# Causal masks carried by the shift and decay matmuls, the early expert table made in PSUM, and a new order of the attention steps

## Chip, cores and metric

One core of a Trainium2 chip runs the whole program. The metric is the device time of one execution in microseconds, lower is better. The kernel before takes 850.12 us (median of 3 runs, 849.7 to 854.04).

## What is computed

Eight batches of eight heads, 576 positions, head size 64, all in float32, then a mixture of eight experts over the 4,608 tokens, each token going to one expert:

```python
scores = scale * np.matmul(q, k.transpose(0, 1, 3, 2))
cum = np.cumsum(log_f, axis=-1)
decay = cum[:, :, :, None] - cum[:, :, None, :]
causal = np.triu(np.ones((S, S), dtype=bool), k=1)
scores = np.where(causal, -1000000000.0, scores + decay)
scores = scores - np.max(scores, axis=-1, keepdims=True)
attn = np.exp(scores)
attn = attn / (np.sum(attn, axis=-1, keepdims=True) + 1e-09)
return np.matmul(attn, v).astype(np.float32)
...
e_idx = np.argmax(logits, axis=1)
for e in range(E):
    h = np.maximum(x[mask] @ w1[e], 0.0)
    out[mask] = gate_w[mask, None] * (h @ w2[e])
```

## The kernel before

**Attention (class `Attn`)** goes by pairs of heads, 32 pairs, four to a batch. The two heads of a pair stand on partitions 0 to 63 and 64 to 127, so each operand of the scores has 64 rows per head and the matmuls of the two heads are issued in turn. Numbers that need more than one 16-bit or reduced-precision term are split into a high and a low part: `split_hi` (line 397, ACT) and `split_lo` (line 403, POOL) of q and k, `half` (line 651, ACT) and `rest` (line 663, DVE or POOL) of the exponentials.

For a pair, `max_mm` (lines 532 to 552) computes scores with the queries on the partitions, in five blocks of 128 queries laid out in four groups, and `max_red` takes the maximum of each row on DVE (lines 561 to 566). Each group has three kinds of matmuls into one PSUM tile: masks first (line 540: a constant 0/1 matrix `id2` times a table `after` with -1e30 above the diagonal), then the decay (line 546: ones `Cq` times `Sk`, whose rows hold -8 times the cumulated logs in three bfloat16 parts), then q times k (line 551). The maxima are transposed on TensorE (line 572), negated and split on DVE (lines 578, 579), and sent by DMA into rows of `Sq` (`shift_out`, line 586). `scores` (lines 590 to 623) has the keys on the partitions, again masks (line 606, `id2` and `later`), then decay and shift in one matmul of `Sk` and `Sq` (line 613), then three products of q and k parts (line 621). A mask group of a block of 128 columns has a 128-column and a 64-column matmul per head. `exp` (lines 630, 636) follows on ACT; `weighted` (lines 689 to 691) multiplies the exponentials with v, 15 times three matmuls per head; `divide` (lines 700 to 705) normalises. `put_cum` (line 412) sends the cumulated logs of a pair into `Sk` by one DMA from SP, `Sk` and `Sq` having three slots in turn. Per batch there are also the scaling of v, the key gates (line 491), the routing (`route`) and the scatter of the tokens into the experts' lists (`scatter`, line 797, an indirect DMA on POOL).

**The order.** Nothing is scheduled by the compiler here: `steps` lists every step with the steps it comes after and with the PSUM and SBUF rings it takes, and `Plan.order` emits, one by one, the ready step with the smallest due time. A step's due time is `PERIOD * b + DUE[kind][stage][q]`, where the stage is batch 0, batch 1, a middle batch or the last one and q the pair within the batch. The engines then run their instructions in that order. The costs given to `add` are not used by the kernel. The tile `pb` is one PSUM bank that the transposes, the key gates and the small matmuls share.

**Setup.** `Moe.__init__` makes the constants of the experts on POOL before `Attn.setup` makes those of attention on DVE, POOL and ACT, computes the cumulated logs (lines 274 to 301) and splits q and k of the first two pairs. `setup2` follows as a step.

**The early table.** After batch 5 (`EB`), `early` (line 1327) counts the tokens of each expert so far (line 996, TensorE), works out on DVE which expert and which rows the first four tiles take (`first_table`, lines 1062 to 1074, with `parts`, `slots` and `table`) and loads two tiles of x. It is one step, after the scatters of batch 5. `other_tables` does the rest during the experts' stage.

**Experts (class `Moe`)**: 14 to 18 tiles of 256 tokens and up to eight of 128, each with two layers as three products of split operands (lines 1211 and 1237), weights loaded and split per expert.

## Time and profile before

| | |
|---|---|
| median of 3 runs | 850.12 us |
| profiled execution | 849.61 us |
| its span, first to last instruction | 847.8 us |
| TensorE busy (mean granted clock 0.983) | 807.1 us, 95% |
| VectorE (DVE) busy | 627.7 us, 74% |
| ScalarE (ACT) busy | 543.2 us, 64% |
| GpSimd (POOL) busy | 378.7 us, 45% |

Times within the profile are microseconds from the first instruction on. A line number is a line of the kernel. Attention fills the first 375 us or so, the experts the rest. In the lists of instructions the columns are start, duration, engine, line, operation, output<-inputs, tile sizes and a count; an arrow in brackets gives the idle time of the engine before the instruction and what ended it. Consecutive instructions of one kind are merged into one line. Matmuls are pipelined, so that a matmul's duration is longer than its distance to the next one.

### The profile page before, as it was taken

The numbers are of one execution on the slowest core, as the hardware profiler recorded it, in microseconds if no ns is written. First come the engines' busy times: TensorE is split into PE (matmuls) and PEld (weight loads), VectorE is DVE, ScalarE is ACT, GpSimd is POOL, SyncE is SP. The second block draws the span as 40 slices with busy tenths as digits, with TensorE's granted clock in tenths as the row PEclk, the third lists the DMA queues.
The fourth block names the chain that finished last, engine by engine and source line by source line (L and its number), as shares of the span: only waits on it lengthen the run. The fifth ranks groups of instructions, "written<-read, shape, count | busy, mean of one in ns | idle before, by whom it ended". The sixth has DMA issues, their size and how long they took to land.

```text
span 847.8 us, 23444 instructions
## 1 busy us (share of the span) xinstructions
PE 807.1 (95%) x9693; PEld 726.9 (86%) x9693; DVE 627.7 (74%) x1170; ACT 543.2 (64%) x688; POOL 378.7 (45%) x370
## 2 busy tenths in 40 slices
PE   3899999999999999699999999999999999999994
PEld 2689898989898988588999999999999999999873
DVE  8679798989898989877777856666655666566484
ACT  4597889898989897474643654444454445444484
POOL 9386889898989897575433111111000110111110
PEclk9699999999999999899999999999999999999997
DMA  5434353535353533171474731101113421116481
GB/s 171 145 104 140 125 182 116 184 116 180 119 182 116 184 115 108 64 244 58 149 249 157 295 121 51 51 27 49 38 51 137 149 67 50 51 44 207 146 299 30
DMA packets 43016, 107.48 MB, mean 127 GB/s; under 512 B 5391, under 2 KB 5583, under 8 KB 42896
## 3 DMA queue, kind: packets, MB, share of 16 engines
q1 hardware_dynamic: 36192, 84.82, 30.1%
q0 software_dynamic: 6704, 21.02, 6.8%
q8 instruction: 80, 1.31, 0.7%
q14 instruction: 40, 0.33, 0.1%
HBM read 143.14 MB, written 21.80 MB: 195 GB/s over the span
## 4 chain that ended last, share of the span: by engine, by line
PE 86%; DVE 7%; POOL 2%; issue 2%; ACT 1%; DMA 0%; DVEq 0%; POOLq 0%; ACTq 0%
PE ph L1211 23%; PE py L1237 23%; PE ps L621 9%; PE pb L491 4%; PE po L689 4%; PE po L691 3%; PE po L690 3%; PE ps L551 3%; PE ps L613 3%; PE ps L546 2%; PE ph L1293 2%; PE ps L606 2%; PE px L1194 2%; PE ps L540 2%; DVE w1l L1157 1%
## 5 line engine op out<-in xcount | busy, mean ns | idle before, releaser
L1242 POOL DMA_INDIRECT out_dram<-y,xg x36 | 48.0, 1334 | 333.7 <-DVE y L1241 304.8
L1211 PE MATMUL ph<-xh,w1h 128*128 128x256 f32 x576 | 163.3, 284 | 0.3 <-DVE hl L1215 0.3
L1211 PE MATMUL ph<-xl,w1h 128*128 128x256 f32 x576 | 163.1, 283 | 0.0
L1211 PE MATMUL ph<-xh,w1l 128*128 128x256 f32 x576 | 162.9, 283 | 0.0
L663 POOL TENSOR_TENSOR Pl<-Pt,Ph 128x1024 f16<-128x1024 f32 (+1 forms) x63 | 142.0, 2260 | 17.9 <-ACT Ph L651 14.4
L1157 DVE TENSOR_TENSOR w1l<-raw,w1h 128x1024 fp32r<-128x1024 f32 x78 | 97.6, 1265 | 61.5 <-ACT w1h L1155 61.5
L1174 ACT CAST w2h<-raw 128x1024 fp32r<-128x1024 f32 x72 | 74.6, 1048 | 95.1 <-issue 55.3
L1155 ACT CAST w1h<-raw 128x1024 fp32r<-128x1024 f32 x80 | 82.5, 1048 | 82.5 <-PE ph L1211 62.5
L1175 DVE TENSOR_TENSOR w2l<-raw,w2h 128x1024 fp32r<-128x1024 f32 x72 | 87.5, 1221 | 58.7 <-ACT w2h L1174 56.9
L1211 PEld LDWEIGHTS ph<-xh,w1h 128*128 128x128 f32 x576 | 110.5, 192 | 1.2 <-DVE hl L1215 0.5
L1237 PE MATMUL py<-w2h,hh 128*128 128x512 f32 x288 | 111.3, 395 | 0.0
L1211 PEld LDWEIGHTS ph<-xl,w1h 128*128 128x128 f32 x576 | 110.5, 192 | 0.7
L1211 PEld LDWEIGHTS ph<-xh,w1l 128*128 128x128 f32 x576 | 110.5, 192 | 0.0
L1237 PE MATMUL py<-w2l,hh 128*128 128x512 f32 x288 | 110.2, 391 | 0.0
L1237 PE MATMUL py<-w2h,hl 128*128 128x512 f32 x288 | 109.9, 391 | 0.0
L621 PE MATMUL ps<-X 64*128 64x288 f32 (+4 forms) x1152 | 109.8, 319 | 0.0
L689 PE MATMUL po<-vh,Ph 128*128 128x73 f16 x930 | 100.3, 199 | 2.1 <-DVE lgh L705 2.1
L403 POOL TENSOR_TENSOR X<-raw,X 128x1152 fp32r<-128x1152 f32 x32 | 84.7, 2649 | 38.5 <-ACT X L397 38.2
L691 PE MATMUL po<-vh,Pl 128*128 128x73 f16 x930 | 99.8, 198 | 1.5 <-DVE Pl L663 1.3
L690 PE MATMUL po<-vl,Ph 128*128 128x72 f16 x930 | 100.1, 196 | 0.0
L689 PEld LDWEIGHTS <-Ph 128*128 128x128 f16 x960 | 93.6, 98 | 5.9 <-issue 2.8
L636 ACT ACTIVATE Pt<-ps,lnp 128x576 f32<-128x576 f32 (+1 forms) x96 | 81.3, 864 | 24.9 <-PE ps L621 24.9
(301 smaller groups left out, 1944.2 us busy)
## 6 DMA issues: line engine op xcount, KB each, us to landing
raw<-in_w_dram SPq DMA_DIRECT2D x84, 1024.0 KB
raw<-in_qk_dram SPq DMA_DIRECT2D x32, 608.0 KB
vT<-in_vt_dram SPq DMA_DIRECT2D x32, 320.0 KB
xg<-xs SPq DMA_DIRECT2D x18, 514.0 KB
vr<-in_v_dram SPq DMA_DIRECT2D x30, 256.0 KB
raw1b<-in_w_dram SPq DMA_DIRECT2D x4, 1024.0 KB
hxg<-xs SPq DMA_DIRECT2D x5, 257.0 KB
vr<-in_v_dram SPq DMA_DIRECT2D x8, 128.0 KB
```

Source lines behind the costliest of these rows:

```text
L403: e.tensor_tensor(self.two(X[:, 1]), self.two(self.get("raw", p)), self.two(f32(X[:, 0])), ALU.subtract)
L621: nc.tensor.matmul(ps[:, h, c0:c0 + w], X[r, x, k], X[r, y, q], start=False, stop=(j == 2), skip_group_check=True)
L636: nc.scalar.activation(self.get("Pt", (p, i))[:, :, o:o + w], ps[:, :, 0:w], AF.Exp, bias=self.lnp, scale=0.125)
L663: e.tensor_tensor(self.Pl_t[p % 2][:, :, c], self.exps(p, i), self.Ph_t[p % 2][:, :, c], ALU.subtract)
L689: nc.tensor.matmul(o, Ph[:, c0:c0 + P], vh[:, c, hh, :], start=(c == 0), stop=False)
L690: nc.tensor.matmul(o[:, 1:73], Ph[:, c0:c0 + P], vl[:, c, hh, :], start=False, stop=False)
L691: nc.tensor.matmul(o, Pl[:, c0:c0 + P], vh[:, c, hh, :], start=False, stop=(c == ic))
L1155: x = nc.scalar.copy(self.w1h[a], self.raw1[i][a])
L1157: y = e.tensor_tensor(self.w1l[a], self.raw1[i][a], f32(self.w1h[a]), ALU.subtract)
L1175: y = nc.vector.tensor_tensor(self.w2l[a], self.raw2[a], f32(self.w2h[a]), ALU.subtract)
L1211: y = nc.tensor.matmul(ph[:, i, :], w[:, k, f0:f0 + P], x[:, k, :], start=(j == 0), stop=(j == len(m) - 1))
L1237: x = nc.tensor.matmul(py, h[:, k, c * P:c * P + P], w[:, k, :], start=(j == 0), stop=(j == len(m) - 1))
```

## The change

The three mask tables and `id2` go. `Sk` gets three versions of its 128 columns, `Cq` three of its 128 and `Sq` further rows: partitions 32 to 63 of each head hold powers of two, chosen so that their products give a large negative number above the diagonal of a block of 64 columns and nothing of weight below. The matmuls of lines 546 and 613 are cut at 64 columns in diagonal blocks, and each part takes the version that masks it; the separate mask matmuls are gone. The logs go into all three versions of a slot: for pair 0 by six DMAs from SBUF, three of them on ACT's queue, for the others by two DMAs that read a copy in DRAM. Slots 1 and 2 of `Sk` and `Sq` are filled by two new steps, on ACT and on POOL. The experts' constants become a step (`setup4`), `setup2` is divided, and its memsets of `vh`, `Ph` and `Pl` move into `setup`. The early table becomes four steps with its operands in the PSUM bank; it needs the routing of batch 5, and only the loads of x wait for the scatters; the "done" counts are worked out in the experts' stage. All due times are new (two kinds are shown).

```diff
-BIG = 1.0e30
+MLOW, MTOP = 2.0 ** -43, 2.0 ** 36
...
-    ('cum',): ((-242.6133, -50.2149, -6.6544, -25.4361,), (-56.0267, -77.1295, -25.7943, 18.3990,), (-19.3542, -20.5147, -34.8776, -48.3972,), (-31.7442, -27.2763, -26.2392, 12.4635,),),
+    ('cum',): ((-341.2901, -70.2974, -16.1453, -104.4206,), (-283.1303, -79.5174, -46.2929, 13.8484,), (-28.1546, -31.8015, -114.5039, -643.4896,), (-70.0973, -16.2522, -27.1466, 6.5397,),),
-    ('sp',): ((-0.3617, 18.9754, 31.7166, 38.9344,), (9.7884, 19.6782, 33.2576, 38.0054,), (10.2387, 18.5857, 29.4347, 38.2310,), (9.6684, 19.0880, 33.0092, 24.8589,),),
+    ('sp',): ((-6.6104, 15.8973, 30.1030, 40.3096,), (6.5407, 16.2118, 28.6304, 40.4840,), (9.2313, 15.7400, 27.2300, 38.0838,), (8.9220, 17.4086, -20.5558, 22.4380,),),
...
+        self.sums = dram.tile([64, 3, S], BF16, name="sums")
...
+        self.Sk, self.Sq = t([P, 3, 3, QW], BF16, "Sk"), t([P, 3, QW], BF16, "Sq")
+        self.Cq, self.keys, self.ques = t([P, 3, P], BF16, "Cq"), t([P, 3, P], BF16, "keys"), t([P, 64], BF16, "ques")
+        flat = lambda x: x.rearrange("p a b -> p (a b)").bitcast(F32)
+        nc.vector.memset(flat(self.keys), 0.0)
+        nc.vector.memset(flat(self.Cq), 0.0)
+        nc.vector.memset(self.ques, 1.0)
+        for x in (0, 64):
+            nc.vector.memset(self.keys[x:x + 3], 1.0)
+            nc.vector.memset(self.keys[x:x + 1], 0.0)
+            nc.vector.memset(self.keys[x:x + 1, 1, 0:64], -MTOP)
+            nc.vector.memset(self.keys[x + 32:x + 33, 1, 64:P], -MTOP)
+            nc.vector.memset(self.Cq[x:x + 6], 1.0)
+            nc.vector.memset(self.Cq[x:x + 3], 0.0)
+            nc.vector.memset(self.Cq[x:x + 1, 2, 0:64], 1.0)
+            nc.vector.memset(self.ques[x:x + 1], 0.0)
+        pos = t([P, 64], F32, "pos")
+        for x in (0, 64):
+            nc.gpsimd.iota(pos[x:x + 64], [[1, 64]], base=-127, channel_multiplier=2, allow_small_or_imprecise_dtypes=True)
+        u1, w1, w2 = t([P, 64], F32, "u1"), t([P, 64], F32, "w1"), t([P, 64], F32, "w2")
+        nc.gpsimd.tensor_scalar(w1, pos, 0.0, -MLOW, ALU.is_equal, ALU.mult)
+        nc.gpsimd.tensor_scalar(w2, pos, 1.0, -MTOP, ALU.is_equal, ALU.mult)
+        for x in (32, 96):
+            nc.gpsimd.tensor_tensor(self.keys[x:x + 32, 1, 0:64], w1[x:x + 32], w2[x:x + 32], ALU.add)
+            nc.gpsimd.tensor_tensor(self.keys[x:x + 32, 2, 64:P], w1[x:x + 32], w2[x:x + 32], ALU.add)
+        nc.gpsimd.tensor_scalar(u1, pos, 0.0, MTOP / MLOW, ALU.is_lt, ALU.mult)
+        nc.gpsimd.tensor_scalar(w2, pos, 0.0, None, ALU.is_equal)
+        for x in (32, 96):
+            for y in (self.Cq[x:x + 32, 1, 0:64], self.Cq[x:x + 32, 2, 64:P], self.ques[x:x + 32]):
+                nc.gpsimd.tensor_tensor(y, u1[x:x + 32], w2[x:x + 32], ALU.add)
...
+        self.queries(nc.gpsimd.tensor_copy, 0)
-        self.id2 = t([P, 2, P], BF16, "id2")
-        self.later = t([P, 2, P], BF16, "later")
-        self.after = t([P, 2, P], BF16, "after")
-        nc.gpsimd.memset(self.id2, 0.0)
-
-        def mask(t, k):
-            nc.gpsimd.memset(t, 0.0)
-            for h in range(2):
-                a = t[64 * h:64 * h + 64]
-                nc.gpsimd.affine_select(a, a, [[64 * k, 2], [-k, P]], ALU.is_ge, -BIG, base=0, channel_multiplier=k)
-        mask(self.after, 1)
...
+        self.rows(nc.scalar.copy, 0)
+        nc.vector.memset(self.vr[64:128, 4, :], 0.0)
...
-        for x in range(2):
-            nc.vector.tensor_tensor(self.id2[:, x, 64 * x:64 * x + 64], self.ident[:, 0:64], self.ident[:, 64:P], ALU.add)
-        nc.gpsimd.memset(self.Sq[:, 0], 1.0)
-        mask(self.later, -1)
-        nc.gpsimd.memset(self.Sq[:, 1:], 1.0)
...
+    def rows(self, copy, i):
+        copy(self.Sk[:, i].rearrange("p v (c n) -> p v c n", n=P),
+             self.keys.rearrange("p v (o n) -> p v o n", o=1).broadcast_to([P, 3, NJ, P]))
+
+    def queries(self, copy, i):
+        copy(self.Sq[:, i].rearrange("p (c n) -> p c n", n=64), self.ques.rearrange("p (o n) -> p o n", o=1).broadcast_to([P, 2 * NJ, 64]))
+
+    def slot(self, i):
+        copy = self.nc.scalar.copy if i == 1 else self.nc.gpsimd.tensor_copy
+        self.rows(copy, i)
+        self.queries(copy, i)
...
-        self.nc.sync.dma_start(self.Sk[3:114:22, p % 3, 0:S], self.chl[2 * p:2 * p + 2])
+        for h, e in enumerate((self.nc.sync, self.nc.scalar if p == 0 else self.nc.sync)):
+            o, u = self.Sk[64 * h + 3:64 * h + 6, p % 3, :, 0:S], 2 * p + h
+            if p:
+                e.dma_start(o, self.sums[u].rearrange("r (o s) -> r o s", o=1).broadcast_to([3, 3, S]))
+            else:
+                for v in range(3):
+                    e.dma_start(o[:, v], self.chl[u:u + 1])
+        if p == 0:
+            self.nc.sync.dma_start(self.sums, self.chl)
...
-        segs = self.SEG[g]
-        masked = [s for s in segs if s[3] + s[1] == MW[s[2]]]
-        first = True
-        for c0, w, ic, j0 in masked:
-            for x, n in ((0, P), (1, 64)) if w > 64 else ((1, 64),):
-                for h in range(2):
-                    r = slice(64 * h, 64 * h + 64)
-                    nc.tensor.matmul(pm[:, h, c0 + w - n:c0 + w], self.id2[r, x], self.after[r, x, P - n:], start=first, stop=False,
-                                     skip_group_check=True)
-                first = False
-        for c0, w, ic, j0 in segs:
+        segs = [(c0, w, ic, j0, 0) for c0, w, ic, j0 in self.SEG[g]]
+        segs = [y for c0, w, ic, j0, _ in segs for y in self.parted(c0, w, ic, j0)]
+        for n, (c0, w, ic, j0, v, q) in enumerate(segs):
             for h in range(2):
                 r = slice(64 * h, 64 * h + 64)
-                nc.tensor.matmul(pm[:, h, c0:c0 + w], self.Cq[r], self.Sk[r, p % 3, j0:j0 + w], start=not masked, stop=False,
+                nc.tensor.matmul(pm[:, h, c0:c0 + w], self.Cq[r, q], self.Sk[r, p % 3, v, j0:j0 + w], start=(n == 0), stop=False,
                                  skip_group_check=True)
-        for c0, w, ic, j0 in segs:
+        for c0, w, ic, j0 in self.SEG[g]:
             for h in range(2):
                 r = slice(64 * h, 64 * h + 64)
                 nc.tensor.matmul(pm[:, h, c0:c0 + w], X[r, 0, QC - 64 + P * ic:QC + 64 + P * ic], X[r, 0, j0:j0 + w],
                                  start=False, stop=True, skip_group_check=True)
+
+    @staticmethod
+    def parted(c0, w, ic, j0):
+
+        if j0 + w != MW[ic]:
+            return [(c0, w, ic, j0, 0, 0)]
+        e = w - 64
+        r = [(c0 + e, 64, ic, j0 + e, 1, 2)]
+        if w > 64:
+            r = [(c0 + e - 64, 64, ic, j0 + e - 64, 2, 1)] + r
+        return ([(c0, w - P, ic, j0, 0, 0)] if w > P else []) + r
...
-            x = self.nc.sync.dma_start(self.Sq[32 * a:P:64, p % 3, :], mT[:, a])
+            x = self.nc.sync.dma_start(self.Sq[1 + a:P:64, p % 3, :], mT[:, a])
...
-        masked = [s for s in segs if s[3] == P * s[2]]
-        first = True
-        for c0, w, c, i0 in masked:
-            for x, n in ((1, P), (0, 64)) if w > 64 else ((0, 64),):
-                for h in range(2):
-                    r = slice(64 * h, 64 * h + 64)
-                    nc.tensor.matmul(ps[:, h, c0:c0 + n], self.id2[r, x], self.later[r, x, 0:n], start=first, stop=False,
-                                     skip_group_check=True)
-                first = False
+        parts = []
         for c0, w, c, i0 in segs:
+            n = 0
+            if i0 == P * c:
+                n = min(w, P)
+                parts += [(c0 + 64 * a, 64, c, i0 + 64 * a, 1 + a) for a in range(n // 64)]
+            if w > n:
+                parts.append((c0 + n, w - n, c, i0 + n, 0))
+        for n, (c0, w, c, i0, v) in enumerate(parts):
             k = slice(KC + P * c, KC + P * c + P)
             for h in range(2):
                 r = slice(64 * h, 64 * h + 64)
-                nc.tensor.matmul(ps[:, h, c0:c0 + w], self.Sk[r, p % 3, k], self.Sq[r, p % 3, 64 + i0:64 + i0 + w],
-                                 start=not masked, stop=False, skip_group_check=True)
+                nc.tensor.matmul(ps[:, h, c0:c0 + w], self.Sk[r, p % 3, v, k], self.Sq[r, p % 3, 64 + i0:64 + i0 + w],
+                                 start=(n == 0), stop=False, skip_group_check=True)
...
-        add("setup2", (), "POOL", 8.0, self.setup2, ())
+        add("slot", (1,), "ACT", 2.3, self.slot, (1,))
+        add("slot", (2,), "POOL", 3.0, self.slot, (2,))
+        add("setup2", (), "POOL", 1.25, self.setup2, ())
+        add("setup3", (), "POOL", 2.95, self.setup3, (), [("setup2",)])
+        add("setup4", (), "POOL", 2.1, lambda: self.others(), (), [("setup3",)])
         add("gs", (), [("DVE", 0.2), ("PE", 0.2), ("DVE", 0.2), ("PE", 0.2), ("DVE", 1.2)], 0, self.gate_scale, (), take=("pb", "gs"),
...
-            add("cum", k, "SP", 0.55, self.put_cum, k, [prev("s", 3, g) for g in range(4)], lands=10e3)
+            add("cum", k, "SP", 1.1, self.put_cum, k, [("slot", p) if p in (1, 2) else None] + [prev("s", 3, g) for g in range(4)], lands=10e3)
...
-            add("early", (), [("PE", 0.2), ("POOL", 0.15), ("DVE", 4.5), ("SP", 2.3)], 0, early, (), [("sc", EB, c) for c in range(NJ)], take=("pb", "e"), free=[("pb", "e")])
+            add("early", (), "PE", 0.25, self.begin_early, (early,), [("setup4",), ("rt", EB, 4)], take=("pb", "e"))
+            add("early1", (), "DVE", 2.0, self.go_early, (), [("early",)])
+            add("early2", (), "DVE", 1.8, self.go_early, (), [("early1",)], free=[("pb", "e")])
+            add("early3", (), "SP", 2.3, self.load_early, (), [("early2",)] + [("sc", EB, c) for c in range(NJ)])
         return plan
 
-    def run(self, early=None):
+    def begin_early(self, early):
+        self.early = early()
+        next(self.early)
+
+    def go_early(self):
+        next(self.early)
+
+    def load_early(self):
+        self.owned("xs", EB)
+        next(self.early)
...
+    def constants(self):
...
-    def first_table(self, n):
+    def done_early(self):
         vec = self.nc.vector
-        nt = self.parts(n, 0, 8, "a")
-        e, k, ok, cum = self.slots(nt, EARLY, None, "a")
-        vec.memset(e[:, 0:1], -1.0)
-        self.last = e[:, EARLY:EARLY + 1]
-        self.row = self.table(e, k, cum, EARLY, "a")
-
+        nt, cum = self.early_counts[:, 0:8], self.early_counts[:, 8:16]
         done = self.done = self.keep.tile([1, 8], F32, name="c_done")
-        vec.tensor_tensor(done, cum[:, 0], nt, ALU.subtract)
+        vec.tensor_tensor(done, cum, nt, ALU.subtract)
...
+        self.done_early()
...
-        self.first_table(self.counts(acc, pc, "a"))
-        for t in range(2):
-            self.load_x(t)
+        self.nc.tensor.matmul(pc[:, 0:8], self.ones, acc, start=True, stop=True)
+        yield
+        vec = self.nc.vector
+        at = 8
+
+        def t(*shape):
+            nonlocal at
+            n = int(np.prod(shape))
+            at += n
+            x = pc[0:1, at - n:at]
+            if len(shape) == 1:
+                return x
+            return x.rearrange("o (a b) -> o a b", b=shape[1])
+        keep = self.keep.tile([1, 16], F32, name="c_early")
+        s1, s3 = [1, EARLY, 1], [1, EARLY, 8]
+        ni = t(8).bitcast(I32)
+        vec.tensor_copy(ni, pc[0:1, 0:8])
+        vec.tensor_scalar(ni, ni, 8, None, ALU.arith_shift_right)
+        e = t(EARLY + 1, 1)
+        vec.memset(e[:, 0:1], -1.0)
+        at_nt = at
+        nt, cum = t(8), t(1, 8)
+        vec.tensor_copy(nt, ni)
+        vec.tensor_tensor_scan(cum[:, 0], nt, self.zeros, 0.0, ALU.add, ALU.add)
+        io = self.io[:, 0:EARLY]
+        base, k = t(EARLY, 1), t(EARLY, 1)
+        le, left = (self.keep.tile([1, EARLY, n], F32, name=f"c_le{n}") for n in (8, 1))
+        vec.tensor_tensor(le, cum.broadcast_to(s3), io.broadcast_to(s3), ALU.is_le)
+        vec.tensor_reduce(e[:, 1:], le, AX.X, ALU.add)
+        vec.tensor_tensor(le, le, cum.broadcast_to(s3), ALU.mult)
+        vec.tensor_reduce(base, le, AX.X, ALU.max)
+        yield
+        vec.tensor_tensor(left, io, base, ALU.subtract)
+        vec.scalar_tensor_tensor(k, e[:, 1:], float(CAP // T), left, ALU.mult, ALU.add)
+        ex = self.keep.tile([1, EARLY + 1, 1], F32, name="c_ex")
+        vec.tensor_copy(ex, e)
+        tab = self.keep.tile([1, 4, EARLY], I32, name="c_taba")
+        part = lambda r: tab[:, r].rearrange("o (n c) -> o n c", c=1)
+        vec.tensor_copy(part(0), e[:, 1:])
+        vec.tensor_copy(part(1), k)
+        ch = t(EARLY, 1)
+        vec.tensor_tensor(ch, e[:, 1:], ex[:, 0:EARLY], ALU.not_equal)
+        x = vec.tensor_copy(part(2), ch)
+        self.tabled = [vec.tensor_copy(tab[:, 3, 0:1], cum[:, 0, 7:8]).ins.name, x.ins.name]
+        vec.tensor_copy(keep[:, 0:16], pc[0:1, at_nt:at_nt + 16])
+        self.row = [tab[0:1, :, i:i + 1] for i in range(EARLY)]
+        self.last = ex[:, EARLY:EARLY + 1]
+        self.early_counts = keep
+        yield
+        for i in range(2):
+            self.load_x(i)
+        yield
```

## Rows read from the trace of the kernel before

**Rows 1.** Busy us by stretch: PE, PEld, DVE, ACT, POOL; clock, DMA share, GB/s

```profile
15.00:46.20 31.20, 27.43 (x316) 22.13 (x316) 22.80 (x49) 18.78 (x26) 16.31 (x16) 0.78 0.41 139
...
88.60:299.70 211.10, 209.44 (x4231) 188.94 (x4230) 183.00 (x453) 185.80 (x238) 182.48 (x164) 1.00 0.47 151
...
341.50:354.70 13.20, 7.37 (x114) 5.99 (x113) 11.14 (x33) 6.79 (x8) 5.34 (x4) 0.74 0.24 81
...
388.00:830.00 442.00, 441.32 (x2804) 400.23 (x2805) 294.83 (x370) 224.74 (x280) 73.39 (x69) 1.00 0.34 118
```

**Rows 2.** The same for line 689 alone: PE, PEld, then clock and DMA

```profile
88.60:299.70 211.10, 64.50 (x600) 58.48 (x600) 1.00 0.47 151
```

**Rows 3.** Chain of waits, 88.6 to 299.7 us: share of it by line

```profile
by line: PE ps L621 23.8%; PE po L689 10.9%; PE pb L491 10.7%; PE po L691 9.6%; PE po L690 9.4%; PE ps L551 7.3%; PE ps L613 6.8%; PE ps L546 6.6%; PE ps L606 4.6%; PE ps L540 4.1%; PE pb L572 2.0%; DVE x L702 1.2%; PE pb L450 0.7%; DVE z L
```

**Rows 4.** Waits, 88.6 to 299.7 us: total us, times, longest

```profile
ACT ps L630 <- PE ps L621: 10.3, 14, 1.2
ACT Pt L636 <- PE ps L621: 9.5, 15, 1.2
```

**Rows 5.** List of TensorE's instructions at the early table

```profile
350.23 0.50 PE L606 MATMUL ps<-later,id 64*128 64x128 bf16 x8 [4.98 <-DVE Pl L663]
```

**Rows 6.** List of DVE's instructions, the early table

```profile
341.79 2.53 DVE L1026 TENSOR_TENSOR c_lea<-c_cuma,c_io 1x32 f32<-1x32 f32 x1
...
346.32 2.32 DVE L1072 TENSOR_SCALAR c_done<-c_done 1x8 f32<-1x8 f32 x1
...
348.95 1.23 DVE L663 TENSOR_TENSOR Pl<-ps,Ph 128x1024 f16<-128x1024 f32 x1
```

**Rows 7.** TensorE's instructions: one pair's mask groups, and the group behind each

```profile
197.60 0.34 PE L540 MATMUL ps<-after,id 64*128 64x128 bf16 x8
197.78 0.38 PE L546 MATMUL ps<-Sk,Cq 64*128 64x192 bf16 x4
...
198.53 0.26 PE L540 MATMUL ps<-after,id 64*128 64x128 bf16 x4
198.62 0.29 PE L546 MATMUL ps<-Sk,Cq 64*128 64x288 bf16 x2
...
201.19 0.29 PE L540 MATMUL ps<-after,id 64*128 64x64 bf16 x6
201.32 0.38 PE L546 MATMUL ps<-Sk,Cq 64*128 64x64 bf16 x4
```

**Rows 8.** List of POOL's instructions at the early table

```profile
341.65 2.63 POOL L403 TENSOR_TENSOR X<-raw,X 128x1152 fp32r<-128x1152 f32 x1
...
346.27 2.36 POOL L663 TENSOR_TENSOR Pl<-Pt,Ph 128x1152 f16<-128x1152 f32 x1 [1.99 <-ACT Ph L651]
```

**Rows 9.** DVE by line, 88.6 to 299.7 us: busy us, mean ns, idle before

```profile
L663 DVE TENSOR_TENSOR Pl<-ps,Ph 128x1024 f16<-128x1024 f32 x20 | 24.1, 1207 | 0.5
```

**Rows 10.** List of instructions, the start (SPq issues DMAs)

```profile
0.82 0.61 SPq L247 DMA_DIRECT2D Pt<-in_f_dram  x1
...
3.68 0.73 DVE L274 TENSOR_SCALAR Pt<-Pt 64x576 f32<-64x576 f32 x1 [0.83 <-DMA Pt<-in_f_dram]
...
5.68 1.15 ACT L397 CAST X<-raw 128x1152 fp32r<-128x1152 f32 x1 [0.55 <-DMA raw<-in_qk_dram]
...
9.64 1.80 SPq L412 DMA_DIRECT2D Sk<-chl  x2
...
10.23 2.99 POOL L403 TENSOR_TENSOR X<-raw,X 128x1152 fp32r<-128x1152 f32 x1
...
15.04 0.39 PE L540 MATMUL ps<-after,id 64*128 64x64 bf16 x6
15.13 1.06 ACT L427 ACTIVATE junk<-vr 128x1024 f16<-128x1024 f32 x1 [4.26 <-issue]
...
27.25 0.38 PE L606 MATMUL ps<-later,id 64*128 64x128 bf16 x4
```

**Rows 11.** Busy us by stretch, after the early table (columns as in rows 1)

```profile
349.00:352.00 3.00, 1.77 (x22) 1.68 (x22) 2.50 (x5) 0.00 (x0) 0.20 (x1) 0.50 0.68 243
```

More of the change, by code (lines that the diff above doesn't have):

```diff
@@ L152 @@
-    ('early',): ((334.4029,),),
+    ('slot',): ((0.0000, -90.2608, -60.5121,),), ('setup2',): ((-42.1805,),), ('setup3',): ((-15.4352,),),
+    ('setup4',): ((1.1573,),), ('gs',): ((-54.8584,),),
+    ('hi',): ((-90.5074, -11.2133, 2.9083, 27.9858,), (-84.1206, -5.6247, 9.2824, -51.9076,), (-225.1714, -685.2260, -13.4921, -314.0636,), (-208.1829, -683.0768, 12.6029, -25.1772,),),
+    ('lo',): ((-24.0068, -17.4806, 4.0965, -30.1911,), (-25.3007, -75.7010, -14.4672, -14.6053,), (-7.4218, -195.1788, 9.9272, 19.2035,), (-8.2839, -195.2343, 16.0830, 34.8736,),),
@@ L292, in setup @@
-        mask(self.after, 1)
+        self.queries(nc.gpsimd.tensor_copy, 0)
+        self.Ph_t = [t([P, 2, PW], F16, f"Ph{i}") for i in range(2)]
+        self.Pl_t = [t([P, 2, PW], F16, f"Pl{i}") for i in range(2)]
+        for x in self.vh:
+            nc.gpsimd.memset(x[:, :, :, 0:1], 1.0)
+            nc.gpsimd.memset(x[64:128, 4, :, 0:1], 0.0)
+        for x in self.Ph_t + self.Pl_t:
+            nc.gpsimd.memset(x[:, :, 1600:], 0.0)
         nc.scalar.activation(ft, ft, AF.Ln)
+        self.rows(nc.scalar.copy, 0)
@@ L840, in steps @@
             for g in range(4):
-                add("s", k + (g,), "PE^", (0.615, 0.535, 1.275, 1.18)[g], self.scores, (p, g), [("so", p), ("lo", p), ("cum", p)],
+                add("s", k + (g,), "PE^", (0.54, 0.535, 1.17, 1.02)[g], self.scores, (p, g), [("so", p), ("lo", p), ("cum", p)],
                     take=("ps", (p, g)))
@@ L848, in steps @@
                 add("h", k + (i,), "ACT", (1.06, 0.9, 0.95)[i], self.half, (p, i),
-                    [("e", p, g) for g in gs] + ([("w", 2 * p - 4), ("w", 2 * p - 3)] if p > 1 else [("setup2",)]))
+                    [("e", p, g) for g in gs] + ([("w", 2 * p - 4), ("w", 2 * p - 3)] if p > 1 else []))
                 add("r", k + (i,), "DVE" if i == 1 or self.is_last(p, i) else "POOL", (1.28 if self.is_last(p, i) else 2.35, 1.14, 2.15)[i], self.rest, (p, i), [("h", p, i)],
@@ L869, in steps @@
             add("v2", k, [("PE", 0.2), ("DVE", 0.6)], 0, self.v_scale, k,
[L870 removed]
+                [("v3", b)] + ([("d", NH * (b - 1) - 1)] if b > 1 else []),
                 take=("pb", ("v2", b)), free=[("pb", ("v2", b))])
@@ L889, in steps @@
                 add("rt", k + (i,), ops, 0, self.route, (b, i), [("ga", b) if i == 0 else ("rt", b, i - 1)])
-            ea = ("early",) if early and b == EB + 1 else None
-            add("rt", k + (4,), [("PE", 0.3), ("DVE", 0.25), ("POOL", 0.25)], 0, self.route, (b, 4), [("rt", b, 3), bp("rt", 1, 4), ea, ("setup2",)],
+            ea = ("early3",) if early and b == EB + 1 else None
+            add("rt", k + (4,), [("PE", 0.3), ("DVE", 0.25), ("POOL", 0.25)], 0, self.route, (b, 4), [("rt", b, 3), bp("rt", 1, 4), ("early",) if ea else None, ("setup2",)],
                 take=("pb", ("r", b)), free=[("pb", ("r", b))])
@@ L1422, in early @@
             def early():
-                for x in ("acc", "xs"):
-                    a.owned(x, EB)
-                moe.early(a.acc, a.bank("c"))
-            a.run(early)
+                a.owned("acc", EB)
+                return moe.early(a.acc, a.bank("c"))
+            a.run(early, moe.constants)
             acc = keep.tile([P, 8], F16, name="c_acc")
```

167 lines of the change are left out of this document (75 added, 92 removed), and 52 rows, old and new, of the table DUE.

## Prediction

> **What bounds the kernel now.** I read the busy times by stretch first. From 88.6 to 299.7 us TensorE is busy 209.4 of 211.1 us at a granted clock of 1.00, while ACT, DVE and POOL are busy 183 to 186 us, 86 to 88% [rows 1]. Busy time of pipelined matmuls says little by itself, so next the pace: line 689 runs 15 times per head and 120 times per batch, and it ran 600 times in that stretch [rows 2], so a batch takes 211.1/5 = 42.2 us. Then the chain of waits there: the lines of TensorE named in its row add up to 96.5%, and lines 606 and 540, the mask matmuls that the change takes out, to 8.7% [rows 3]. Last the waits: ACT, the busiest of the others, waited 10.3 + 9.5 us for the scores matmuls [rows 4], 4.0 us a batch, which is most of its idle time. So attention is TensorE's, with the others some five us a batch behind. The experts' stage (388 to 830 us) is TensorE's too, 441.3 of 442.0 us [rows 1]; none of its matmuls changes.
>
> One stretch is neither: between 341.5 and 354.7 us TensorE was busy 7.4 us of 13.2, its clock 0.74 on the mean [rows 1]. That stretch begins and ends with the start of one head's po matmuls; at the pace of 42.2/8 = 5.3 us a head, 7.9 us were lost. The long wait there names DVE, line 663, 4.98 us [rows 5]; on DVE that instruction came at 348.95 us [rows 6], behind the small instructions of the early table.
>
> **The masks, 32 pairs of heads.** Removed per pair: 18 mask matmuls before the maxima and 18 before the scores. Their price is the distance from a mask group's start to the start of the group behind it: 0.18 (x8), 0.09 (x4) and 0.13 us (x6) for the maxima [rows 7], 0.40 us; the same three sizes stand before the scores, so 0.80 us a pair. Two heads run side by side on half the rows each, so the columns of one head count: 384, 192 and 256, which at 2.4 GHz are 0.347 us. The other 0.053 us over 18 instructions is 3 ns for each. Added: the Cq and the Sk matmuls are cut at 64 columns in the diagonal blocks, 28 in place of 12 per phase, with the same columns in all. At 3 ns each, 16 more cost 0.05 us a phase, and 0.70 us a pair remain saved. The ends: 0.80 if a cut is free, and 0.10 if every matmul costs 0.40/18 = 22 ns whatever its width. I take 0.70, since the three sizes follow their columns.
>
> Over 32 pairs that is 22 us of TensorE's work. It becomes time only as far as the others keep up. In the steady stretch TensorE would want 42.2 - 4 x 0.70 = 39.4 us a batch; ACT needs 185.8/5 = 37.2, DVE and POOL 36.5 to 36.6 [rows 1]. Ends: 2.8 us a batch (all of it), and 0.8 us (ACT, in a fixed order, takes over at 90% busy). I take 1.9, nearer the upper end since the chain names hardly anything but TensorE. From 46.2 to 341.5 us are 7.0 batches: **13.3 us** (5.6 to 19.6).
>
> **The early table.** It works on tiles in SBUF. Two of its instructions took 2.53 and 2.32 us for 32 and 8 elements, and each ended when a POOL instruction did: 344.32 beside POOL's 344.28, and 348.64 beside 348.63 [rows 6, 8]. Line 663 on DVE, with one operand in PSUM, takes 1.21 us on the mean [rows 9] in a stretch where POOL is busy 86% [rows 1]: such a form is not held. The change puts the small operands in PSUM and splits the work into two steps on DVE; the four instructions of "done" move into the experts' stage, beside a TensorE that is busy throughout (without that cover under 1 us); only the loads of x on SP still wait for the scatters. Some 19 instructions remain, at some 0.2 us each 4 us in two pieces, of which I let 1.5 reach TensorE: **6.4 us** of the 7.9 (2 to 8). The one small PSUM bank stays taken from the matmul to the second piece, and the transposes of the maxima queue behind it on TensorE; that is in the 1.5. The Trainium skill ("SBUF — State Buffer", section "Who interferes with whom") says that DVE is shut out by a POOL instruction when it has two SBUF inputs or runs in a two-port mode. By it nothing is held any more and the term stands; if DVE were held beside POOL in every form, it would be rival 5.
>
> **The start.** Off POOL go the experts' constants (to a later step) and the building of two masks; off DVE goes `id2`; the zeros of vr go from POOL to DVE. On come a copy of 1920 columns on ACT, then slots of 2560 columns, one on ACT and one on POOL, some 16 small POOL instructions, eight memsets from setup2, and DMAs: cum(0) is three on SP and three on ACT's queue, then the sums go to DRAM, and from pair 1 on two reads of them replace one copy. ACT: 1152 columns take 1.15 us [rows 10], so 1.9 us come before cum(0) and 2.6 after; the second lies in ACT's idle 4.26 us [rows 10]. Two issues of cum on SP took 1.80 us from 9.64 on, 0.9 each; f, issued at 0.82, let DVE go at 3.68, some 2.9 us to land [rows 10]. ACT's three then start at about 11.7, the last at 13.5, and land at about 16.4 at the most; the first maxima matmul was at 15.04 [rows 10]: about 1 us late. Pair 1 waits for the sums: 9.64 + 4 x 0.9 + 2.9 + 2.9 = 19.0, about when TensorE gets there; behind that wait on SP stands the last part of v, for whose maximum ACT waits. POOL's slot, up to 5.8 us at line 403's rate, stands ahead of the first subtraction, done at 13.2 before, and the first scores were at 27.25 [rows 8, 10]: hidden. In return the masks of the first four pairs go, 2.8 us warm, in a stretch with the clock at 0.78 on the mean [rows 1]. Net **2 us** (5 gained to 3 lost).
>
> **The end.** Pairs 30 and 31 lose their masks too, but other engines share that chain: **1 us** (0 to 2). The second issue of cum per pair, up to 0.9 us of SP in some 10.5, I cost at nothing: it lies beside attention, and rival 4 is its price without that cover.
>
> **Sum.** 13.3 + 6.4 + 2 + 1 = 22.7. The profiled execution took 849.6 us (span 847.8 and 1.8 around it), 0.5 under the median of the runs. 849.6 - 22.7 = 826.9, say **827 us**.
>
> **Rivals.**
> 1. *Everything passes*: 19.6 us in steady attention, the rest as above, 820.6 us. For it: 96.5% of the chain. Against: the four engines stand within 3 us a batch of each other. 0.17.
> 2. *Another engine is the bound at once* (ACT, or POOL, which waits for ACT): 5.6 in place of 13.3, 834.6 us. For it: the 88%. 0.14.
> 3. *Matmuls are paid by the piece.* Per pair 60 become 56; at 22 ns that is 0.09 us, 3 us in all: 849.6 - 3 - 6.4 - 1 = 839 us. Against it: the three group sizes. 0.06. The Trainium skill ("TensorE: Matmul & The Clock Gate", section "Back-to-back issue gap") states a sustained 81 ns for a matmul of 128 columns with its weight load, more than the columns take; by that figure the saving would be an estimated 4 x 81 ns, 0.3 us a pair. The trace's 22 ns disagree with it.
> 4. *The shift comes late: slower.* Each pair's shift goes to Sq over the SP queue that cum is on. If the added issue (up to 0.9 us) stands ahead of it and TensorE has nothing else, 32 x 0.9 = 29 us come on top: 827 + 29 = 856 us. It decides from 22.7/32 = 0.7 us a pair on. Against it: SP has room, and TensorE has po matmuls of other heads to do. 0.05.
> 5. *The early chain stalls as before*: 827 + 6.4 = 833 us. 0.08.
>
> **How the numbers follow.** The forecast has 0.46, and alone the range 820 to 834. Rivals 1, 2, 3 and 5 are gains too, 0.45 together. 0.04 is left for an order that gives it all back (850). So faster 0.91, same 0.04, slower 0.05, the bound being 0.5% (4.2 us), about what a measurement of this kernel can tell from no change. The range 814 to 841 takes in rivals 1 to 3 and 5 with the start and the early table at their ends, and leaves out some 0.15.
>
> **What would show it.** Right: the lines of the masks gone; 120 po matmuls of line 689 in about 40.3 us; ACT over 90% and waiting less than 4 us a batch for scores; no DVE instruction of the early table over 0.4 us, no 5 us wait of TensorE there, the clock at 1.00; the first maxima matmul between 14 and 17 us. Wrong: a batch still at 42 us with TensorE busy (the cuts cost what the masks did), or with TensorE idle behind ACT, POOL or the landing of Sq; or the clock lost in the steady stretch, as after the 5 us wait, when it was 0.50 for 3 us [rows 11].

## The result, and the profile after

The changed kernel takes 841.47 us (median of 4 runs, 840.59 to 843.40) where the kernel before took 851.51 in the same comparison: ratio 0.9883, interval 0.9848 to 0.9918. It is faster by 1.2%, where the prediction had 2.7% (827 us). The side was right; the time is just outside its range (814 to 841). The profiled span is 838.8 us, 9.0 less than before. The starts of the heads' first po matmuls (line 689 before, 715 after) split those 9.0 us by stretch:

| stretch | before | after | gained | predicted |
|---|---|---|---|---|
| start of the span to the first po matmul | 46.2 | 44.7 | 1.5 | 2 |
| six batches of eight heads | 253.5 | 249.6 | 3.9 | 11.4 (6 x 1.9) |
| from there to the last head (with the early table) | 76.0 | 71.9 | 4.1 | 9.3 (1.9 + 6.4 + 1) |
| from there to the end (experts) | 472.1 | 472.6 | -0.5 | 0 |

The busy times by stretch (PE, PEld, DVE, ACT, POOL, then the clock, DMA share and GB/s) answer to [rows 1]: five batches, the early table, the experts.

```profile
85.20:294.30 209.10, 205.24 (x4153) 183.61 (x4152) 185.61 (x454) 185.22 (x238) 182.47 (x164) 1.00 0.46 153
333.00:346.00 13.00, 10.64 (x152) 8.90 (x152) 11.74 (x43) 5.88 (x8) 10.93 (x11) 0.74 0.25 83
388.00:830.00 442.00, 438.38 (x2780) 396.88 (x2778) 293.88 (x367) 224.78 (x279) 66.23 (x57) 1.00 0.34 116
```

TensorE now idles 3.9 us in five batches (1.7 before), and ACT is at 88.6%, not over 90%. The waits of the same five batches (total, times, longest) show that ACT waits for scores as long as before [rows 4], that POOL, in its order, waits for ACT's copies of q and k, for 16.0 us (18.1 before), and that TensorE has a new wait, for VectorE in the chain of v's maximum:

```profile
POOL X L419 <- ACT X L413: 16.0, 11, 2.2
ACT Pt L662 <- PE ps L647: 10.5, 14, 1.4
ACT ps L656 <- PE ps L647: 9.1, 15, 1.1
...
PE pb L474 <- DVE a L468: 3.4, 5, 0.8
```

TensorE's list, one maxima group and one scores group of a pair. The cut Cq or Sk matmuls come first, then the q.k matmuls behind them; PEld is the list of weight loads of the same stretch.

```profile
196.87 0.40 PE L562 MATMUL ps<-Sk,Cq 64*128 64x64 bf16 x8
197.11 0.56 PE L567 MATMUL ps<-X 64*128 64x64 f32 x4
197.51 0.40 PE L639 MATMUL ps<-Sq,Sk 64*128 64x64 bf16 x8
197.74 1.10 PE L647 MATMUL ps<-X 64*128 64x448 f32 x12
```

```profile
196.87 0.28 PEld L562 LDWEIGHTS <-Cq 64*128 64x128 bf16 x8
197.08 0.30 PEld L567 LDWEIGHTS ps<-X 64*128 64x128 f32 x4
197.50 0.17 PEld L639 LDWEIGHTS <-Sk 64*128 64x128 bf16 x8
197.71 1.02 PEld L647 LDWEIGHTS ps<-X 64*128 64x128 f32 x12
```

A maxima group lasts 0.64 us here (197.51 - 196.87), and from its first cut matmul to the first q.k matmul pass 0.24 us. Taken over all pairs and for the same neighbours, the six groups of a pair became shorter by 78, 29 and -1 ns (maxima) and 108, 105 and 34 ns (scores): 0.35 us a pair, not 0.70.

On DVE's list, the early table [rows 6] has none of its old stalls, but its end ("done") runs in attention, at 337.82 us, although the kernel calls it in `other_tables` (line 1126), in the experts' stage; so not every instruction stands where the order of the steps puts it. One instruction of it takes 2.49 us; POOL's list beside it:

```profile
337.63 0.15 DVE L1420 COPY c_early<-pb 1x16 f32<-1x16 f32 x1
337.82 0.15 DVE L1117 TENSOR_TENSOR c_done<-c_early 1x8 f32<-1x8 f32 x1
...
338.43 2.49 DVE L1120 TENSOR_SCALAR c_done<-c_done 1x8 f32<-1x8 f32 x1
340.84 1.27 DVE L588 TENSOR_REDUCE mt<-ps 128x2 f32<-128x128 f32 x2
```

```profile
338.26 2.64 POOL L419 TENSOR_TENSOR X<-raw,X 128x1152 fp32r<-128x1152 f32 x1
```

Both end at 340.9 us, and a maxima reduction stood behind.

### The profile page after: what moved, and what is told of

It reads as the page before. It is cut to its first block, busy times and chain, and to the rows that moved or that the text cites. A ratio compares the mean times of both kernels' runs of the same rounds, so it can differ in the third digit from the quotient of the medians.

```text
span 838.8 us, 23294 instructions
## 1 busy us (share of the span) xinstructions
PE 800.2 (95%) x9565; PEld 718.1 (86%) x9565; DVE 623.3 (74%) x1177; ACT 547.8 (65%) x691; POOL 382.6 (46%) x376
## 4 chain that ended last, share of the span: by engine, by line
PE 86%; DVE 7%; ACT 2%; issue 2%; DMA 1%; POOL 0%; ACTq 0%; DVEq 0%
PE ph L1258 23%; PE py L1284 23%; PE ps L647 9%; PE pb L515 4%; PE po L715 4%; PE ps L567 4%; PE po L717 3%; PE po L716 3%; PE ps L639 3%; PE ps L562 3%; PE ph L1340 2%; PE px L1241 2%; DVE w1l L1204 1%; DVE mt L588 1%; PE pb L599 1%
## 5 line engine op out<-in xcount | busy, mean ns | idle before, releaser
L715 PEld LDWEIGHTS <-Ph 128*128 128x128 f16 x960 | 93.7, 98 | 6.1 <-DVE lgh L731 1.5
L716 PEld LDWEIGHTS <-Ph 128*128 128x128 f16 x960 | 94.6, 99 | 0.8 <-issue 0.5
```

Of the source, the lines that this page charges most:

```text
L715: nc.tensor.matmul(o, Ph[:, c0:c0 + P], vh[:, c, hh, :], start=(c == 0), stop=False)
L716: nc.tensor.matmul(o[:, 1:73], Ph[:, c0:c0 + P], vl[:, c, hh, :], start=False, stop=False)
```

## Experiments

A "steady batch" below is the mean of the fourth to sixth batch of eight heads, from the starts of their po matmuls: 42.2 us before, 41.8 after. Each run without an interval is one profiled execution. A steady batch repeats well: it is 41.8 us in the change, e8, e11 and e16, which differ only in other places, and 42.2 in the kernel before and e4.

**1. What a cut costs on TensorE.** e1_wide_last sorts the pieces of a group so that the widest stands last, ahead of the q.k matmuls. e2_no_cut leaves out the masks and the cuts (and takes the decay logs at a tenth); the tokens then go to other experts, so only attention compares.

```diff
+        segs.sort(key=lambda s: s[1])      # max_mm
+        parts.sort(key=lambda s: s[1])     # scores
```

> The changed kernel with the parts of each Cq and Sk group sorted so that the widest matmul stands last, ahead of the first q times k matmul; the same matmuls otherwise. Theory 'uncovered load': the 187 ns weight load of the float32 operand behind a 64-column matmul stands open for some 90 ns. Then the groups shrink: maxima 192/320 from 583 to about 500 ns, 64/448 from 633 to about 550, scores 448/64 from 1,178 to about 1,100, 320/192 from 1,077 to about 1,020, masked 288 from 580 to about 535; 0.35 us a pair, and if TensorE is still what sets the pace, a batch goes from 41.8 to about 40.4 us and the run gains some 9 us. Theory 'price of a cut': every cut matmul costs some 10 ns by itself wherever it stands; then no group changes by more than 10 ns and the time by less than 1 us.

> The changed kernel without cuts: Cq and Sk matmuls at full width with version 0, so no mask at all is applied, and the logs scaled to a tenth so that nothing overflows. It shows the floor of TensorE without masks. Theory 'uncovered load' and theory 'price of a cut' both expect groups as the prediction summed them: maxima 192/320 near 480 to 500 ns, 64/448 near 530, scores 448/64 near 1,100, 320/192 near 1,020. If TensorE sets the pace: a batch at about 40 us and 10 to 12 us less than the changed kernel. If the order of the other engines' work sets it: a batch still at 41 us or more.

e1: 842.81 us (4 runs), ratio 0.9897 (0.9851 to 0.9943), no faster than the change as it was. TensorE's list and its weight loads, the same two groups:

```profile
197.19 0.40 PE L563 MATMUL ps<-Sk,Cq 64*128 64x64 bf16 x8
197.32 0.58 PE L568 MATMUL ps<-X 64*128 64x64 f32 x4
197.74 0.40 PE L641 MATMUL ps<-Sq,Sk 64*128 64x64 bf16 x8
197.87 1.13 PE L649 MATMUL ps<-X 64*128 64x448 f32 x12
```

```profile
197.29 0.33 PEld L568 LDWEIGHTS ps<-X 64*128 64x128 f32 x4
```

The maxima group now lasts 0.55 us (197.74 - 197.19; 0.64 in the change), the scores group behind it 1.10 (1.17), as the theory "uncovered load" had it; by "price of a cut" neither would have moved. Over all pairs and like neighbours the six groups are 0.31 us a pair shorter than in the change and 0.66 shorter than before, near the 0.70 of the prediction. So it is the last piece that was mis-priced. The reading of it, which no row shows directly: a 64-column piece is over long before the fp32 weight load behind it, some 0.19 us by PEld's list, is done; a wide one covers that load. TensorE gets lighter (200.88 us busy in 208.00, from 205.24 in 209.10), but the steady batch goes only from 41.8 to 41.5 us, and without any cut (e2: 814.46 us in all, with 445.8 for the experts) it is 41.5 too. From there on something else sets the pace.

**2. What is next.** e14_before_no_masks drops the mask matmuls of the kernel before, with nothing in their place. e5, e6 and e7 take e1 and leave half the columns out of one engine's copies or subtractions of the probabilities (two of three parts on ScalarE, two on GpSimd, one on VectorE); e13 and e15 do GpSimd's part in the changed kernel and in the kernel before.

```diff
         # rest(); for half() the same with "and i"
+        n = (c.stop - c.start) // 2 if 2 <= p < 28 and i != 1 else c.stop - c.start
+        k = slice(c.start, c.start + n)
-        e.tensor_tensor(self.Pl_t[p % 2][:, :, c], self.exps(p, i), ...
+        e.tensor_tensor(self.Pl_t[p % 2][:, :, k], self.exps(p, i)[:, :, 0:n], ...
```

> The kernel before without its mask matmuls at all (the decay logs at a tenth, so that the outputs stay finite; other numbers, so only the attention compares), old order, uncut parts: TensorE loses 0.80 us per pair, 3.2 per batch. If TensorE alone set the pace, as the prediction took it: 39.0 to 39.8 us per batch. If another engine was right behind it: 41.0 to 41.6, what e3_old_order shows with the new masks in the same order.

> Base: the changed kernel with the widest piece last (e1_wide_last), whose batches of eight heads take 41.5 us although TensorE is busy only 200.9 of 208 us. Here ScalarE rounds only half the columns of two of the three parts of a pair's probabilities (2 x 1024 elements become 2 x 512) for pairs 2 to 27, about 0.95 us less for ScalarE per pair, 3.8 per batch; the rest of the columns keep an older pair's values, so the outputs are other numbers and the experts' stage may differ; only the batches of the attention compare. If ScalarE sets the pace now: a batch of 39.5 to 40.5 us (TensorE's own floor takes over). If VectorE or GpSimd sets it: 41.5. If it is the order itself (each engine waits its turn in a ring of short waits): 41.0, a part of what is removed.

> Base e1_wide_last. GpSimd subtracts only half the columns in its two parts of each pair's remainders, pairs 2 to 27: about 2.2 us less for GpSimd per pair, 8.8 per batch. If GpSimd sets the pace: 39.5 to 40.5 us per batch. If ScalarE or VectorE does: 41.5. If the order: 41.0 or so.

> Base e1_wide_last. VectorE subtracts only half the columns of its part of each pair's remainders, pairs 2 to 27: about 0.6 us less for VectorE per pair, 2.4 per batch. If VectorE sets the pace: 39.5 to 40.5 us per batch. If ScalarE or GpSimd does: 41.5. If the order: 41.0 or so.

> The changed kernel as it is, with half the columns of GpSimd's remainders left out for pairs 2 to 27 (8.8 us less for GpSimd a batch). If GpSimd binds in the changed kernel: 40.4 to 41.0 us per batch, TensorE busy over 98%. If TensorE with its uncovered weight loads binds there: 41.5 to 42.0, as in the changed kernel.

> The kernel before with half the columns of GpSimd's remainders left out for pairs 2 to 27. If TensorE alone bound it: 42.2 us per batch, unchanged. If GpSimd had a part: 41.5 or less.

Steady batch: e14 41.2, e5 41.5, e6 **40.6**, e7 41.5, e13 41.3, e15 42.2 us. In all they took, in this order, 813.09 (fewer us for the experts), 843.51, 833.27, 834.42, 845.25 and 849.49 us; e7's gain lies in its start and its end, not in its pace. Busy times of four batches of e5, e6 and e7, one fence each, and of e14:

```profile
85.00:253.00 168.00, 163.06 (x3362) 145.75 (x3362) 148.87 (x370) 138.70 (x196) 147.17 (x132) 1.00 0.46 153
```

```profile
85.00:253.00 168.00, 165.20 (x3460) 148.37 (x3458) 151.19 (x379) 153.82 (x200) 115.47 (x138) 1.00 0.48 159
```

```profile
85.00:253.00 168.00, 162.82 (x3383) 145.45 (x3383) 143.83 (x369) 151.20 (x194) 148.57 (x132) 1.00 0.47 157
```

```profile
86.00:250.00 164.00, 157.83 (x2806) 140.09 (x2803) 145.40 (x361) 148.05 (x191) 145.76 (x130) 1.00 0.48 153
```

e14 is the run that decides: without the masks TensorE's groups are 0.73 us a pair shorter, 2.9 a batch, but the batch falls by 1.0, and TensorE idles 6.2 us in 164. The second bound lay 1 us behind TensorE, not 5. With the widest piece last it is GpSimd, in its own order: only its lighter queue moves e1 (41.5 to 40.6, and TensorE is then busy for 165.2 of 168 us, 98.3%), although it was busy only 87% and waited 16.6 us in five batches for ACT's copies of q and k. Halving ScalarE's or VectorE's share changes nothing; by the busy times that took 2.7 and 1.7 us a batch from them (7.6 from GpSimd), more than the 0.9 gained. One rival is left: a lighter GpSimd also holds VectorE less. VectorE's subtraction for v (line 541, two inputs in SBUF) took 0.96 us on the mean in four batches of e1 and 0.74 in e6, 1.1 us a batch. That e7 gained nothing speaks against it, but no run separates the two. Nor was GpSimd tried as the second bound in the order of before (e14). In the change as it is, GpSimd accounts for 0.5 (e13: 41.8 to 41.3) and TensorE, busy 98.9% in e13, for the rest; in the kernel before it had no part (e15).

**3. Masks or order.** e3_old_order is the changed kernel with the due times of before, e12_new_order_old_masks the kernel before with the new ones. The edit is the table of due times.

> The changed kernel with the due times of the kernel before wherever a step exists in both. Theory 'the new order gives part of it back' (1.8 more changes a batch between the half-row matmuls and the full ones, and 0.7 us more waiting): a batch takes about 41.0 us, since the groups are 1.4 us a batch shorter than before. Theory 'the other engines set the pace': a batch stays at 41.8 us or is longer.

> The kernel before (its masks, its early table in SBUF) with the due times of the changed one. If the new order brings the steady gain: batches of 41.6 to 41.9 us, as in the changed kernel. If the masks bring it: 42.2 or more, as before, since the order was searched for other durations.

e3: steady batch 41.6 us (the first three 41.0 to 41.2), but 81.1 us from the seventh batch to the last head (52.9 + 28.2), and 851.76 us in all. e12: 43.0 a batch, 83.2 at the end (58.2 + 25.0), 857.15 us. The steady gain is the masks', not the order's: the new order by itself costs 0.8 us a batch with the old masks (43.0 to 42.2) and 0.2 with the new. The order, which fits the changed kernel alone, is worth 9 us around the early table.

**4. The early table.** e4_before_early is the kernel before with the table in PSUM alone, e8_sbuf_table the changed kernel with its rows back in SBUF.

```diff
-            x = pc[0:1, at - n:at]
+            x = tb[:, at - n:at]           # e8: tb is a tile in SBUF
```

> The kernel before with the early table alone as in the change: operands in PSUM, two steps on DVE, done later. Theory 'shared port': the stretch from the start of the po matmuls at 299.7 us to the end of attention's (74.6 us before) becomes 5 to 7 us shorter and the run takes 843 to 845 us; no DVE instruction of the table over 0.4 us. Theory 'the table's place in the order costs what the port did': 2 us or less.

> The changed kernel with the early table's small rows in SBUF instead of PSUM, its order of steps kept. If PSUM was worth what the prediction gave it: the stalls of the small VectorE instructions behind GpSimd come back (one to three of 1.2 to 2.6 us) and the last two batches (first head of batch 6 to the last head, 72.0 us in the changed kernel) take 76 to 80. If the new order alone, which has the table at another place, brought the gain there: 71 to 73.

e4: 79.0 us for batch seven and the last heads (76.0 before), 852.54 in all. No small DVE instruction of the table is held, yet TensorE waits 4.64 us. Its list names no releaser; the wait ends 0.11 us after the table's last read of the one small bank (line 1391, done at 341.66 us), into which the matmul writes, so it is read as a wait for that bank:

```profile
341.77 2.28 PE L497 MATMUL pb<-gv,vT 128*128 128x16 f32 x10 [4.64 <-issue]
```

e8: 77.3 us (44.7 + 32.6) against 72.0, and 848.79 in all. Its list of DVE has the stalls of before again (2.06, 2.53 and 2.28 us; two of them here):

```profile
339.01 2.06 DVE L1398 CAST c_tb<-c_tb 1x8 f32<-1x8 int32 x1
...
343.06 2.53 DVE L1420 COPY c_early<-c_tb 1x16 f32<-1x16 f32 x1
```

So by this execution PSUM is worth 5.3 us in the new order, and nothing in the order of before, where the key-gate matmuls stand in the bank's way. The rows of the stalls are the firmer evidence: this stretch also took 76.0 us in e13, whose table and order are the change's.

What was still missing was sought first in TensorE's wait of 0.72 us right ahead of the table's matmul, behind which its granted clock falls to 0.50 (1.2 of 2.4 GHz). e11_early_filled moves a maxima group in front of it.

```diff
-    ('mm', 1): (... (-8.2575, 12.0480, 20.1134, 24.7147,),),
+    ('mm', 1): (... (-8.2575, 12.0480, 20.1134, 26.8,),),
```

> The changed kernel with one maxima group of the last pair moved behind the last key-gate matmuls, ahead of the early table's matmul, which in the changed kernel waits 0.7 us for the bank with nothing else to do, right before the granted clock falls to one half for 6.8 us. If the wait is what costs the clock: no stretch at 0.50 at 333 to 341, and the two last batches (72.0 us) take 68 to 70. If the clock falls for another reason (the key-gate matmuls themselves): still 6 to 7 us at 0.50 and 71 to 73.

A miss: the wait moved to the key-gate matmuls (1.2 us), the clock fell all the same (0.50 from 336 to 342 us), the end took 75.1 us (46.6 + 28.5). The stall of "done" was there too, 2.21 us. e16_done_psum works "done" in PSUM right behind the table; e17_wide_done does it with the widest piece last.

```diff
+        d = t(8)                           # early(), in the bank
+        vec.tensor_tensor(d, cum[:, 0], keep[:, 0:8], ALU.subtract)
+        vec.tensor_scalar(d, d, -1.0, float(EARLY), ALU.mult, ALU.add)
+        vec.tensor_tensor(d, d, keep[:, 0:8], ALU.min)
+        vec.tensor_scalar(keep[:, 8:16], d, 0.0, None, ALU.max)
...
-        vec.tensor_copy(e[:, 0:1], self.last)
+        vec.scalar_tensor_tensor(e[:, 0], left[:, 0:1], 0.0, self.last[:, 0], ALU.mult, ALU.add)
```

> The changed kernel with the four instructions of the table's end (line 1117 to 1120) worked in PSUM right behind the second piece of the early table, and one copy of the experts' table tied to a late operand, so that no small instruction with SBUF operands alone stands in VectorE's queue there. If the one stall of 2.49 us is what is missing of the early table's gain: batch 6 and the last heads take 68 to 70 us instead of 72.0, and the kernel 837 to 839 in the median. If the waits for the bank and the fallen clock come without it too: 71 to 73, and 841.

> The same with the widest piece last. e1_wide_last took 75.5 us for batch 6 and the last heads and 842.8 us in the median. If the stall is what costs: 72 to 73, and 837 to 840. If not: 75 and 842.

e16: 839.29 us (6 runs, 837.30 to 841.59), ratio 0.9886 (0.9849 to 0.9923); the profiled one took 69.8 us (44.6 + 25.2) where the change took 72.0. Its ratio is nearly that of the change (0.9883), so in the whole time no gain shows. e17: **833.84 us** (6 runs, 831.10 to 835.47), ratio 0.9813 (0.9777 to 0.9849): faster than both kernels, every run of it below every run of the change and of e1, whose interval (0.9851 to 0.9943) lies above it. Its list of DVE at "done", and busy times by stretch there:

```profile
334.34 0.16 DVE L1418 TENSOR_TENSOR pb<-pb,c_early 1x8 f32<-1x8 f32 x1
334.54 0.16 DVE L1419 TENSOR_SCALAR pb<-pb 1x8 f32<-1x8 f32 x1
334.74 0.16 DVE L1420 TENSOR_TENSOR pb<-pb,c_early 1x8 f32<-1x8 f32 x1
334.93 0.15 DVE L1421 TENSOR_SCALAR c_early<-pb 1x8 f32<-1x8 f32 x1
```

```profile
327.00:341.00 14.00, 11.41 (x208) 9.90 (x207) 11.54 (x46) 7.14 (x11) 11.18 (x11) 0.88 0.23 78
```

The batch with the table and the last heads take 68.9 us (43.7 + 25.2), against 75.5 in e1; the clock there is 0.88 on the mean (0.74 in the change). e1's lighter TensorE had shown no gain because it was given back at this place: 1.5 us gained over six batches, 3.6 lost here. Part of that is the clock's: TensorE was granted 1.2 GHz here for 13.6 us in e1, 6.8 in the change and 3.4 in e16 and e17; how much of the gain came that way was not separated.

**5. GpSimd made lighter in earnest, a miss.** e9_route_dve and e10_wide_route move the router's small operations from GpSimd to VectorE.

```diff
-            nc.gpsimd.tensor_tensor(d, lg, m.broadcast_to(s3), ALU.subtract)
+            nc.vector.tensor_tensor(d, lg, m.broadcast_to(s3), ALU.subtract)
...
-            nc.gpsimd.tensor_tensor(oh, self.iota_v, self.get("rei", b).broadcast_to(s3), ALU.subtract)
-            nc.gpsimd.tensor_scalar(oh16, oh, 0.0, None, ALU.is_equal)
+            nc.vector.tensor_tensor(oh16, self.iota_v, self.get("rei", b).broadcast_to(s3), ALU.is_equal)
```

> The changed kernel with the router's small operations moved from GpSimd to VectorE (seven GpSimd instructions of 0.20 to 0.37 us per batch, 1.9 us in sum, and the waits for VectorE between them, become four of about 0.2 us on VectorE; one small one stays); the widest piece is not moved. If GpSimd's queue, in order, is what holds the changed kernel's batches at 41.5 to 42.0 us: 40.8 to 41.2 per batch and about 835 us. If TensorE still binds in this form (1.0 to 1.4 us of waits a batch): 41.5 and 840.

> The same move of the router's operations on top of e1_wide_last. If GpSimd's queue is what keeps e1_wide_last at 41.5 us although TensorE is lighter: 40.5 to 41.0 per batch, five batches of it, and 832 to 837 us. If GpSimd is held by something else than its own work (the order of the steps): 41.5 and 841.

Both are slower: 868.46 us, ratio 1.0235 (1.0172 to 1.0299), and 868.11, ratio 1.0212 (1.0155 to 1.0270); batches of 44.8 to 49.8 us in e9 from the second on. The moved subtraction, in e9's list of one line (ns: least, median, most), takes 2.6 us for 40 columns:

```profile
L757 DVE TENSOR_TENSOR rd<-lg,rm x8: 201/2638/2805, 81.1 to 403.3; 128x40 f32<-128x40 f32 x8
```

Each time VectorE's queue stands still, and the maxima behind it; the granted clock fell six times for 3.4 us each in e9's attention. One of them, with POOL's instruction beside it, ended at 130.5 us as that did:

```profile
127.74 2.81 DVE L757 TENSOR_TENSOR rd<-lg,rm 128x40 f32<-128x40 f32 x1
```

```profile
128.35 2.13 POOL L689 TENSOR_TENSOR Pl<-Pt,Ph 128x1024 f16<-128x1024 f32 x1
```

The Trainium skill ("SBUF — State Buffer", section "Who interferes with whom") says that a VectorE instruction with two SBUF inputs, or one such as tensor_scalar in a two-port mode, contends with GpSimd; these rows and line 1120 above agree. Both expectations left it out of account.

## Why the prediction was wrong

- **The pass-through is the step that failed**: "2.8 us a batch ... 0.8 ... I take 1.9, nearer the upper end since the chain names hardly anything but TensorE", 13.3 us over seven batches (the lower end, ACT at 90%, comes to 42.2 - 37.2/0.9 = 0.9). The chain names what is bound now, not how far behind the next bound is. That was read off the busy shares (86 to 88%, "some five us a batch behind"), and e14 measured 1.0 us in the steady batches, 7.8 over six: with the masks gone at no cost, no more came through in that order. Measured over six batches: 3.9 us. Of 2.9 us a batch less for TensorE 1.0 came through (e14), of 2.6 in e1 0.7, of 1.4 in the change 0.4: about a third, not two thirds. The new order, which the prediction gave no price, took part of that. Rival 2 (another engine is the bound at once, POOL among its two names) had the mechanism, with 0.14.
- **The masks**: removal nearly as priced (0.73 us a pair for 0.80, e14), but "at 3 ns each, 16 more cost 0.05 us a phase" was mis-sized: the saving was 0.35 us a pair in place of 0.70. Cuts of the same columns are near free only when a wide piece stands last (0.66 in e1). Alone this is the smaller step: put right in e1, it took the steady batch only from 41.8 to 41.5 us, where 40.3 was predicted. Rival 3 (matmuls paid by the piece) would have left 0.09.
- **The early table**: the mechanism held (e8: the stalls come back with SBUF; 5.3 of 6.4 us). The step that failed is "the four instructions of 'done' move into the experts' stage, beside a TensorE that is busy throughout": they ran in attention at 337.82 us, with SBUF operands, and one was held for 2.49 us. The clock did not stay at 1.00 there either: 0.50 for 6.8 us (6.9 before). With "done" put right (e16, one execution), the stretch gained 6.2 us where 9.3 were predicted, 1.9 of these from the pass-through. That the bank is held was foreseen and put in the 1.5; under the old order it ate the whole gain (e4).
- **The start**: 1.5 of 2. The first maxima matmul was at 14.14 us, as predicted. The term can't be told from chance: in kernels that do the first pairs as the change does, the first po matmul came between 44.7 and 48.1 us (e13), and with the widest piece last between 41.5 (e7) and 45.5 us (e1).
- **The rest** held: the lines of the masks are gone, no 5 us wait, no late shift (rival 4), the experts within 0.5 us. With 3.9 us for the steady batches and 4.1 for the last stretch, 22.7 becomes the 9.0 of the spans.

## What to carry to other kernels

Before a saving on the bound engine is priced, measure what lies behind: a run that leaves that work out altogether (here the masks, without regard to the outputs) gives the most that leaving out that work can bring in that order; busy shares of 86 to 88% did not show it here, where queues run in order. Where matmuls are cut, let a wide piece stand ahead of an fp32 weight load (0.31 us a pair here). Look where instructions that "move to a later stage" are really issued, and keep small VectorE instructions whose operands are all in SBUF away from a busy GpSimd.
